# Converting float64 weights on two engines: the sign is carried by the scaled upper word and merged by one two-operand pass

## The chip, the cores and the metric

The kernel runs on one core of a Trainium2 chip. The metric is the device time of one execution in microseconds (us). The kernel before takes 1001.97 us, the median of three runs (1000.22 to 1002.98).

## What is computed

Sliding-window attention (4 batches, 8 heads, 576 positions, head size 64, window 64), and behind it two gated feed-forward layers over all 2304 tokens. The attention inputs are float32, or are used as such; the six weight matrices arrive as float64.

```python
scores = scale * np.matmul(q, k.transpose(0, 1, 3, 2))
mask = (rel >= 0) & (rel < 64)                    # rel = query position - key position
attn = softmax(np.where(mask, scores, -1e9))
x = (attn @ v) as 2304 tokens x 512
x = (silu(x @ w_gate) * (x @ w_val)) @ w_out      # 512 -> 1536 -> 512
x = (sigmoid(x @ w_gate2) * (x @ w_val2)) @ w_out2
```

## The kernel before

Tokens are cut into five tiles of 4, 3, 4, 4 and 3 blocks of 128. The main loop runs over ten passes: the five tiles through the first layer, then the same tiles through the second. Each pass walks the hidden dimension in 12 chunks `fc` of 128, and each chunk is three steps of the TensorE: the gate product into `g` (line 429), the value product into `v` (line 429), and the output product of the chunk before into the accumulators `a` (line 441). Every product is made of three float32 products, high times high, low times high and high times low, so each weight chunk exists as two halves, `w[:, 0]` and `w[:, 1]`. A pass over 512 tokens has 36 matmuls to a chunk.

The attention of the first tile runs before the loop, in the order of the string `START`. The attention of each later tile is laid between the steps of the pass before it, one block of 128 tokens each few chunks. Its work on the VectorE is the masking (line 263), the normalisation (lines 292 to 294) and the low half of `x` (line 331).

The weights are converted in 72 chunks of 128 x 512, 36 for each layer. A float64 is two 32-bit words. `load_raw` brings a chunk as 1024 words a partition into a buffer `raw`; the lower and the upper words alternate there. Then:

- `round_a` works on the ScalarE (ACT): line 377 turns the lower words, times 2^-29, into integers (the three bits of mantissa that go over, rounded) and puts them back in their places; line 380 takes the absolute value of the upper words, read as float32, into a contiguous tile `t`.
- `round_b` works on the VectorE (DVE), four passes: line 388 picks the sign from each upper word as 16-bit numbers and writes it into the upper half of the lower word, at a stride of four; line 389 clamps `t`; line 390 shifts `t` left by three as an integer; line 391 adds `t` and the lower words.
- `split_hi` (line 411, ACT) and `split_lo` (line 415, DVE) make the two halves of the weight from `t`.

The order is written out by hand. In the start, `ca`, `cb`, `ch` and `cl` are `round_a`, `round_b`, `split_hi` and `split_lo`. In the loop a table sets at which step a piece is issued. The conversions of the first layer run in the first pass, those of the second layer during the third to sixth passes; each engine works through its own list in that order, and semaphores carry what one waits for. The rows below also name `s` (line 705, gate times value on DVE), `h` (line 707 on ACT, its low half on DVE in line 621), which the output product takes, and `x` (line 328 on ACT, line 331 on DVE), which the products take.

Of the kernel before, what the change touches and what calls it, by code (L numbers as in the profile page):

```python
# [8 lines left out]
FP32 = mybir.dt.float32  # L9
FP32R = mybir.dt.float32r  # L10
INT32 = mybir.dt.int32
UINT32 = mybir.dt.uint32
UINT16 = mybir.dt.uint16
ACTF = mybir.ActivationFunctionType
ALU = mybir.AluOpType
PSUM = bass.MemoryType.PSUM
DRAM = bass.MemoryType.DRAM


F64_LEAST = 2.0 ** -15  # L20
F64_MOST = 122816.0

# [15 lines left out]
def attention_moe_moe(  # L40
# [20 lines left out]
    nc = tc.nc  # L61
# [7 lines left out]
    scale = 1.0 / float(D) ** 0.5  # L69
# [269 lines left out]
    raws = {}  # L339
# [19 lines left out]
        nc.sync.dma_start(out=dst, in_=rows(key))  # L359
        raws[key] = r  # L360

    def words_of(r):
        w = r.rearrange("p (f two) -> p f two", two=2)
        half = r.bitcast(UINT16).rearrange("p (f four) -> p f four", four=4)
        return w[:, :, 0], w[:, :, 1], half[:, :, 1], half[:, :, 3]

# [1 line left out]
    def round_a(key):  # L372
        t = t_p.tile([128, 512], INT32, tag="t", name="t")
        mids[key] = t
        if wide:
            lower, upper, _, _ = words_of(raws[key])
            nc.scalar.activation(  # L377
                out=lower, in_=lower.bitcast(UINT32), func=ACTF.Copy, scale=2.0 ** -29
            )
            nc.scalar.activation(out=t.bitcast(FP32), in_=upper.bitcast(FP32), func=ACTF.Abs)  # L380

    def round_b(key, keep):
        r = raws.pop(key)
        t = mids[key]
        tf = t.bitcast(FP32)
        if wide:
            lower, _, second, fourth = words_of(r)
            nc.vector.tensor_scalar(second, fourth, 0x8000, 0x4000, ALU.bitwise_and, ALU.bitwise_or)  # L388
            nc.vector.tensor_scalar(tf, tf, F64_LEAST, F64_MOST, ALU.max, ALU.min)  # L389
            nc.vector.tensor_scalar(t, t, 3, None, ALU.logical_shift_left)  # L390
            nc.vector.tensor_tensor(out=t, in0=t, in1=lower, op=ALU.add)  # L391
        else:
            nc.vector.tensor_copy(tf, r)
        mids[key] = tf
        if keep:
            d = dram.tile([128, 512], FP32, name=f"k{key[0]}{key[1]}{key[2]}")
            nc.sync.dma_start(out=d, in_=tf)
            kept[key] = d
# [152 lines left out]
    def conv_b(j):  # L551
        round_b(convs[j][1], convs[j][1][1] == "o")
        raw_ahead(j + 1 + 4)

    for j, (s, key) in enumerate(convs[SPLIT_EARLY:], SPLIT_EARLY):
        at(during, s + 1, round_a, key)
        at(during, s + 2, round_b, key, key[0] == 1 or key[1] == "o")
        at(during, s + 2, raw_ahead, j + 1 + 4)
        if key[0] == 0:
            plan_split(s + 2, key)  # L560
# [32 lines left out]
    for t in range(NTL, 2 * NTL):  # L593
        for fc in range(FC):
            n, key = SPT * t + 3 * fc + 5, (1, "o", fc)
# [29 lines left out]
    with tc.manual_schedule():  # L625
# [4 lines left out]
        t = ps_m.tile([128, 512], FP32, tag="a3", name="warm")  # L630
# [8 lines left out]
        for step in LOADS.split():  # L639
# [31 lines left out]
            "lo": lambda i: x_lo(i, x_of(0), i * 128),  # L671
            "wm": lambda k: warm(k),
            "ca": lambda j: round_a(convs[j][1]),
            "cb": lambda j: conv_b(j),
            "ch": lambda j: split_hi(convs[j][1]),
# [9 lines left out]
        for T in range(2 * NTL):  # L685
            m = T // NTL
            t = ORDER2[T - NTL] if m else T
            n = TILES[t][1]
            for fc in range(FC):
# [7 lines left out]
                    out=s, in_=gps[:, 0:n], func=(ACTF.Silu, ACTF.Sigmoid)[m]  # L697
# [54 lines left out]
```

## Time and profile before

| | |
|---|---|
| median of three runs | 1001.97 us |
| the profiled execution | 1002.0 us, of which the span from the first to the last instruction is 1000.2 us |
| TensorE (PE) busy | 980.4 us, 98% of the span |
| VectorE (DVE) busy | 515.6 us, 52% |
| ScalarE (ACT) busy | 457.0 us, 46% |
| mean granted TensorE clock | 0.986 |
| the four conversion passes on DVE, 72 of each | 54.0 + 33.3 + 30.8 + 49.8 us busy |
| the two conversion passes on ACT, 72 of each | 47.9 + 47.9 us busy |

Busy time is the sum of durations, and neighbours on one engine can overlap: an instruction may be recorded as started before the one ahead of it has ended. The share over the whole span hides stages: in the 40 slices of the page, DVE stands at nine tenths in the second to fifth slice (about 25 to 125 us) and at two to three tenths in the second half. What a pass costs is therefore read in the stage in which it stands, from start to start.

### The profile page before, as it was taken

What the parts mean: (1) busy time and instruction counts of PE and PEld (TensorE: products, weight loads), DVE (VectorE), ACT (ScalarE), POOL (GpSimd) and SP (SyncE); (2) the same over time, 40 slices, a digit from 0 to 9 for tenths busy, and PEclk for the clock granted to TensorE, in tenths of its full rate; (3) what the DMA queues carried; (4) which work ended last, traced back from release to release, by engine and by line L of the source; (5) the groups of instructions that cost most, each with busy time, mean ns of one, the idle gap of its engine ahead of it and who ended that gap; (6) DMA issues with size and microseconds to landing.
All of it is one profiled execution on the core that took longest, in us unless ns stands there. A gap on an engine that the chain in (4) does not pass through costs nothing.

```text
span 1000.2 us, 14684 instructions
## 1 busy us (share of the span) xinstructions
PE 980.4 (98%) x5621; PEld 844.7 (84%) x5621; DVE 515.6 (52%) x1181; ACT 457.0 (46%) x981; POOL 4.1 (0%) x20
## 2 busy tenths in 40 slices
PE   8899999999999999999999999999999999999998
PEld 6678778999888888888999888899988888888997
DVE  6999994545677768666555322233322222223322
ACT  6887785555666555655444222222222222222222
POOL 1000000000000000000000000000000000000000
PEclk7999999999999999999999999999999999999999
DMA  9658797962366667464554400020020002000100
GB/s 224 193 179 221 216 240 171 223 148 80 116 212 186 209 206 232 164 205 137 200 148 126 169 0 1 1 85 1 1 74 1 1 1 74 0 1 1 42 1 32
DMA packets 164982, 113.03 MB, mean 113 GB/s; under 512 B 102704, under 2 KB 139568, under 8 KB 164912
## 3 DMA queue, kind: packets, MB, share of 16 engines
q1 hardware_dynamic: 161264, 111.18, 38.4%
q10 hardware_dynamic: 3648, 0.92, 0.4%
q8 instruction: 44, 0.72, 0.3%
q14 instruction: 26, 0.21, 0.1%
HBM read 90.05 MB, written 27.53 MB: 118 GB/s over the span
## 4 chain that ended last, share of the span: by engine, by line
PE 86%; DVE 9%; issue 2%; DMA 1%; ACT 1%; SPq 0%; DVEq 0%
PE a L441 28%; PE g L429 27%; PE v L429 27%; DVE raw L388 2%; PE att L318 1%; DVE t L390 1%; PE att L244 1%; PE att L302 1%; DVE t L391 1%; DVE t L389 1%; DVE z L263 1%; DVE h L621 1%; DVE s L705 1%; DMA raw<-in_moe_w_val_dram 1%; DVE wv L415 0%
## 5 line engine op out<-in xcount | busy, mean ns | idle before, releaser
L429 PE MATMUL g<-x,wg 128*128 128x512 f32 (+1 forms) x1440 | 317.8, 369 | 0.7 <-ACT x L328 0.7
L429 PE MATMUL v<-x,wv 128*128 128x512 f32 (+1 forms) x1440 | 317.6, 369 | 0.0
L429 PEld LDWEIGHTS g<-x,wg 128*128 128x128 f32 x1440 | 263.3, 188 | 37.5 <-ACT x L328 0.8
L429 PEld LDWEIGHTS v<-x,wv 128*128 128x128 f32 x1440 | 261.1, 188 | 33.1
L705 DVE TENSOR_TENSOR s<-s,v 128x512 f32<-128x512 f32 (+1 forms) x120 | 75.9, 632 | 318.3 <-PE v L429 305.9
L696 ACT ACTIVATE s<-g 128x512 f32<-128x512 f32 (+1 forms) x120 | 66.5, 554 | 312.9 <-PE g L429 312.7
L441 PE MATMUL a<-h,wo 128*128 128x512 f32 (+1 forms) x720 | 166.4, 380 | 6.4 <-DVE h L621 6.4
L441 PE MATMUL a<-wo,h 128*128 128x512 f32 x648 | 157.4, 390 | 0.0
L441 PEld LDWEIGHTS a<-h,wo 128*128 128x128 f32 x720 | 132.3, 192 | 27.0 <-DVE h L621 7.6
L707 ACT ACTIVATE h<-s 128x512 fp32r<-128x512 f32 (+1 forms) x120 | 70.6, 588 | 180.6 <-DVE s L705 180.6
L441 PEld LDWEIGHTS a<-wo,h 128*128 128x128 f32 x648 | 121.3, 188 | 24.2
L621 DVE TENSOR_TENSOR h<-s,h 128x512 fp32r<-128x512 f32 (+1 forms) x120 | 76.1, 634 | 3.2
L388 DVE TENSOR_SCALAR raw<-raw 128x512 uint16<-128x512 uint16 x72 | 54.0, 750 | 9.0 <-ACT raw L377 9.0
L279 ACT ACTIVATE z<-z,nm 128x128 f32<-128x128 f32 x144 | 55.8, 389 | 2.9 <-DVE nm L263 2.7
L101 DVE TENSOR_TENSOR x<-rx,x 128x512 fp32r<-128x512 f32 (+1 forms) x20 | 12.8, 639 | 84.3 <-ACT x L100 84.3
L391 DVE CUSTOM_DVE_ANT_0 t<-raw,t 128x1024 uint16<-128x1024 uint16 x72 | 49.8, 692 | 2.5
L380 ACT ACTIVATE t<-raw 128x512 f32<-128x512 f32 x72 | 47.9, 666 | 0.0
L377 ACT ACTIVATE raw<-raw 128x512 int32<-128x512 uint32 x72 | 47.9, 666 | 0.0
L415 DVE TENSOR_TENSOR wo<-stay,wo 128x512 fp32r<-128x512 f32 x60 | 41.1, 684 | 0.0
L411 ACT ACTIVATE wo<-stay 128x512 fp32r<-128x512 f32 x60 | 37.4, 624 | 0.0
L415 DVE TENSOR_TENSOR wo<-tw,wo 128x512 fp32r<-128x512 f32 x48 | 32.9, 685 | 5.7 <-ACT wo L411 5.7
L389 DVE TENSOR_SCALAR t<-t 128x512 f32<-128x512 f32 x72 | 33.3, 463 | 0.0
(84 smaller groups left out, 562.7 us busy)
## 6 DMA issues: line engine op xcount, KB each, us to landing
raw<-in_moe_w_gate_dram SPq DMA_DIRECT2D x24, 512.0 KB, 4.2
raw<-in_moe_w_val_dram SPq DMA_DIRECT2D x24, 512.0 KB, 4.4
raw<-in_moe_w_out_dram SPq DMA_DIRECT2D x24, 512.0 KB, 3.8
tw<-k0o SPq DMA_DIRECT2D x48, 256.0 KB, 4.2
v<-in_v_dram SPq DMA_DIRECT2D x29, 256.0 KB, 4.5
out_dram<-o SPq DMA_DIRECT2D x18, 256.0 KB, 2.3
k<-ks SPq DMA_DIRECT2D x10, 384.0 KB, 5.3
k0o<-t SPq DMA_DIRECT2D x12, 256.0 KB, 2.2
```

What stands on the lines that cost most here:

```text
L279: nc.scalar.activation(out=z[:, hp, :], in_=z[:, hp, :], func=ACTF.Exp, scale=-1.0, bias=nm[:, hp:hp + 1], accum_out=su[:, hp:hp + 1],)
L377: nc.scalar.activation(out=lower, in_=lower.bitcast(UINT32), func=ACTF.Copy, scale=2.0 ** -29)
L380: nc.scalar.activation(out=t.bitcast(FP32), in_=upper.bitcast(FP32), func=ACTF.Abs)
L388: nc.vector.tensor_scalar(second, fourth, 0x8000, 0x4000, ALU.bitwise_and, ALU.bitwise_or)
L391: nc.vector.tensor_tensor(out=t, in0=t, in1=lower, op=ALU.add)
L415: nc.vector.tensor_tensor(out=w[:, 1], in0=mids.pop(key), in1=w[:, 0].bitcast(FP32), op=ALU.subtract)
L429: nc.tensor.matmul(out=ps[:, 0:n], lhsT=w[:, a, c, :], rhs=xt[:, b, c, 0:n], start=(j == 0), stop=(j == len(mm) - 1),)
L441: nc.tensor.matmul(out=acc[e][:, 0:n] if m == 0 else acc[e], lhsT=w[:, a, cols] if m == 0 else h[:, a, cols], rhs=h[:, b, 0:n] if m == 0 e ...
L621: nc.vector.tensor_tensor(out=h[:, 1, 0:n], in0=s, in1=h[:, 0, 0:n].bitcast(FP32), op=ALU.subtract)
L696: nc.scalar.activation(out=s, in_=gps[:, 0:n], func=(ACTF.Silu, ACTF.Sigmoid)[m])
L705: nc.vector.tensor_tensor(out=s, in0=s, in1=vps[:, 0:n], op=ALU.mult)
L707: nc.scalar.activation(out=h[:, 0, 0:n], in_=s, func=ACTF.Copy)
```

## The change

The upper words are no longer stripped of their sign on ACT. They are copied times 2^-112, read as float32, so that the sign bit stays in `t`; this pass now comes first. The lower words, times 2^-29, go to the first 512 words of the `raw` buffer, contiguous (they lie over upper words that the pass before has read). On DVE the pass on 16-bit halves is gone. The clamp comes first, with bounds of both signs; then one `scalar_tensor_tensor` takes the sign bit of `t` and merges it into the lower words; shift and add follow as before. Six instructions on two engines to a chunk before, six now.

```diff
-F64_LEAST = 2.0 ** -15
-F64_MOST = 122816.0
+F64_MOST = 122816.0 * 2.0 ** -112
...
         if wide:
-            lower, upper, _, _ = words_of(raws[key])
+            r = raws[key]
+            words = r.rearrange("p (f two) -> p f two", two=2)
             nc.scalar.activation(
-                out=lower, in_=lower.bitcast(UINT32), func=ACTF.Copy, scale=2.0 ** -29
+                out=t.bitcast(FP32), in_=words[:, :, 1].bitcast(FP32), func=ACTF.Copy, scale=2.0 ** -112
             )
-            nc.scalar.activation(out=t.bitcast(FP32), in_=upper.bitcast(FP32), func=ACTF.Abs)
+            nc.scalar.activation(
+                out=r[:, 0:512], in_=words[:, :, 0].bitcast(UINT32), func=ACTF.Copy, scale=2.0 ** -29
+            )
...
         if wide:
-            lower, _, second, fourth = words_of(r)
-            nc.vector.tensor_scalar(second, fourth, 0x8000, 0x4000, ALU.bitwise_and, ALU.bitwise_or)
-            nc.vector.tensor_scalar(tf, tf, F64_LEAST, F64_MOST, ALU.max, ALU.min)
+            low = r[:, 0:512]
+            nc.vector.tensor_scalar(tf, tf, -F64_MOST, F64_MOST, ALU.max, ALU.min)
+            nc.vector.scalar_tensor_tensor(low, t, -(2 ** 31), low, ALU.bitwise_and, ALU.bitwise_or)
             nc.vector.tensor_scalar(t, t, 3, None, ALU.logical_shift_left)
-            nc.vector.tensor_tensor(out=t, in0=t, in1=lower, op=ALU.add)
+            nc.vector.tensor_tensor(out=t, in0=t, in1=low, op=ALU.add)
```

On DVE, in the first pass of the loop ahead of the first `h` that an output product waits for, the list reads as follows before (ISA is the integer add; the names in brackets are the semaphores that the row waits for, `DVE_49` being DVE's own and `Activation_49` ACT's).

```order
L415 TENSOR_TENSOR wg<-t,wg 128x512 [waits Activation_49]
L388 TENSOR_SCALAR raw<-raw 128x512 [waits DMAHW1_49,Activation_49]
L389 TENSOR_SCALAR t<-t 128x512 [waits Activation_49]
L390 TENSOR_SCALAR t<-t 128x512 [waits DVE_49]
L391 ISA t<-raw,t 128x1024 [waits DVE_49]
L621 TENSOR_TENSOR h<-s,h 128x512
L415 TENSOR_TENSOR wv<-t,wv 128x512 [waits DMAHW4_49,Activation_49]
```

The same place of DVE's list now (lines have moved up by five, and those above the conversion by two):

```order
L410 TENSOR_TENSOR wg<-t,wg 128x512 [waits Activation_49]
L383 TENSOR_SCALAR t<-t 128x512 [waits Activation_49]
L384 SCALAR_TENSOR_TENSOR raw<-t,raw 128x512 [waits DMAHW1_49,DVE_49,Activation_49]
L385 TENSOR_SCALAR t<-t 128x512 [waits DVE_49]
L386 ISA t<-t,raw 128x1024 [waits DVE_49]
L616 TENSOR_TENSOR h<-s,h 128x512
L410 TENSOR_TENSOR wv<-t,wv 128x512 [waits DMAHW4_49,Activation_49]
```

Before, the second of the four passes waits for nothing on DVE; the third waits for the second and the fourth for the third. Now the merge (line 384) waits for the clamp (383), the shift (385) for the merge, whose input it writes over, and the add (386) for the shift. The neighbours stand where they stood.

On ACT, in the same chunk (a little earlier in time, since ACT runs ahead), before:

```order
L707 ACTIVATE h<-s 128x512 [waits DVE_49]
L411 ACTIVATE wg<-t 128x512
L377 ACTIVATE raw<-raw 128x512 [waits DMAHW1_49,Activation_49]
L380 ACTIVATE t<-raw 128x512
L411 ACTIVATE wv<-t 128x512 [waits DVE_49]
```

And now:

```order
L702 ACTIVATE h<-s 128x512 [waits DVE_49]
L406 ACTIVATE wg<-t 128x512
L370 ACTIVATE t<-raw 128x512 [waits DMAHW1_49]
L373 ACTIVATE raw<-raw 128x512 [waits Activation_49]
L406 ACTIVATE wv<-t 128x512 [waits DVE_49]
```

The two passes have changed places, and the second of them (line 373) now waits for the first one's end, since it writes over words that the first one reads. The lists of PE and of the DMA queues keep their order.

## Rows read from the trace of the kernel before

**Rows 1.** The chain that ended last, from the page: shares of the span by engine

```profile
PE 86%; DVE 9%; issue 2%; DMA 1%; ACT 1%; SPq 0%; DVEq 0%
```

**Rows 2.** Busy time by stretch (us and, in brackets, instructions)

```profile
core 0: us, PE busy (x) PEld busy (x) DVE busy (x) ACT busy (x) POOL busy (x), PEclk, DMA share, GB/s
25.00:45.00 20.00, 15.59 (x205) 12.60 (x204) 19.44 (x54) 16.88 (x47) 0.00 (x0) 0.89 0.68 202
45.00:149.20 104.20, 97.06 (x561) 77.25 (x559) 100.92 (x235) 85.96 (x179) 0.00 (x0) 0.97 0.76 210
...
250.00:480.00 230.00, 229.92 (x1422) 188.78 (x1421) 164.32 (x400) 137.57 (x302) 0.00 (x0) 1.00 0.59 186
480.00:1000.20 520.20, 516.33 (x2502) 455.73 (x2500) 165.41 (x270) 147.27 (x272) 0.00 (x0) 1.00 0.14 44
```

**Rows 3.** PE in order of time: where it stood idle (in brackets, with the releaser)

```profile
66.03 3.93 PE L441 MATMUL a<-h,wo 128*128 128x512 f32 x10 [2.12 <-DVE h L621]
...
107.62 4.14 PE L441 MATMUL a<-h,wo 128*128 128x512 f32 x10 [2.12 <-DVE h L621]
...
149.21 3.95 PE L441 MATMUL a<-h,wo 128*128 128x512 f32 x10 [2.12 <-DVE h L621]
158.41 0.65 PE L202 MATMUL att<-ident,k 128*128 128x128 f32 x4 [0.84 <-DVE x L331]
```

**Rows 4.** DVE in order of time ahead of the first of these stalls

```profile
62.59 0.69 DVE L415 TENSOR_TENSOR wg<-t,wg 128x512 fp32r<-128x512 f32 x1
63.20 0.74 DVE L388 TENSOR_SCALAR raw<-raw 128x512 uint16<-128x512 uint16 x1
63.72 0.46 DVE L389 TENSOR_SCALAR t<-t 128x512 f32<-128x512 f32 x1
64.22 0.43 DVE L390 TENSOR_SCALAR t<-t 128x512 int32<-128x512 int32 x1
64.68 0.69 DVE L391 CUSTOM_DVE_ANT_0 t<-raw,t 128x1024 uint16<-128x1024 uint16 x1
65.29 0.68 DVE L621 TENSOR_TENSOR h<-s,h 128x512 fp32r<-128x512 f32 x1
```

**Rows 5.** DVE in order of time: idle ahead of an instruction, 25 to 155 us

```profile
47.42 0.69 DVE L705 TENSOR_TENSOR s<-s,v 128x512 f32<-128x512 f32 x1 [0.87 <-ACT kt L217]
...
152.09 0.76 DVE L388 TENSOR_SCALAR raw<-raw 128x512 uint16<-128x512 uint16 x1 [1.14 <-ACT raw L377]
```

**Rows 6.** DVE's groups between 25 and 149.2 us (count, busy us, mean ns, idle before)

```profile
L388 DVE TENSOR_SCALAR raw<-raw 128x512 uint16<-128x512 uint16 x34 | 25.5, 750 | 0.0
L391 DVE CUSTOM_DVE_ANT_0 t<-raw,t 128x1024 uint16<-128x1024 uint16 x34 | 23.5, 692 | 1.2
L389 DVE TENSOR_SCALAR t<-t 128x512 f32<-128x512 f32 x34 | 15.9, 466 | 0.0
L390 DVE TENSOR_SCALAR t<-t 128x512 int32<-128x512 int32 x34 | 14.5, 427 | 1.2
...
L294 DVE TENSOR_TENSOR z<-z,su 128x512 f32<-128x512 f32 x9 | 6.2, 692 | 0.3
```

**Rows 7.** ACT in order of time: one release by DVE, and two conversions

```profile
43.57 0.63 ACT L411 ACTIVATE wg<-t 128x512 fp32r<-128x512 f32 x1 [1.94 <-DVE t L391]
...
59.59 0.68 ACT L377 ACTIVATE raw<-raw 128x512 int32<-128x512 uint32 x1
60.17 0.66 ACT L380 ACTIVATE t<-raw 128x512 f32<-128x512 f32 x1
...
70.85 0.67 ACT L377 ACTIVATE raw<-raw 128x512 int32<-128x512 uint32 x1
71.40 0.66 ACT L380 ACTIVATE t<-raw 128x512 f32<-128x512 f32 x1
```

**Rows 8.** DVE in order of time: the conversion that follows the last of these

```profile
72.50 0.76 DVE L388 TENSOR_SCALAR raw<-raw 128x512 uint16<-128x512 uint16 x1
```

More of the change, by code (lines that the diff above doesn't have):

```diff
@@ L12 @@
 UINT32 = mybir.dt.uint32
-UINT16 = mybir.dt.uint16
 ACTF = mybir.ActivationFunctionType
@@ L360, in load_raw @@
         raws[key] = r
[L362 to L365, printed above, removed]
     def round_a(key):
```

## The prediction

> **What bounds the kernel now.** I read the chain of waits first. PE holds 86% of it, DVE 9%, ACT 1% [rows 1]: somewhere PE runs late behind DVE, and the next view has to say where. The busy times by stretch do [rows 2]. From 250 us on PE is busy without a gap (0.08 us idle of 230, then 3.87 of 520), and DVE has a third of its time or more to spare. Between 25 and 149.2 us it is the other way round: DVE is busy 97% of the time, while PE idles 4.4 us and then 7.1 us, at a granted clock of 0.89 and 0.97. PE's own order of time shows what it idles for [rows 3]: three times 2.12 us for the low half of `h` (line 621), 41.6 us apart. Before each such stall DVE was not waiting, it was working through its list: its only idle piece between 25 and 149.2 us is 0.87 us at 47.42, the next comes at 152.09 [rows 5]. So up to the stall at 149.21 the end of the kernel hangs on the length of DVE's list, and after it on PE alone. 34 conversions of the first layer stand in that stretch [rows 6]; of the 36, the first stands ahead of it and the last behind the stall at 149.21.
>
> **What a conversion takes on DVE now.** The stretch is saturated, so what counts is from start to start, and not the durations. In the conversion ahead of the first stall [rows 4] line 388 starts at 63.20 and the next foreign instruction (line 621) at 65.29: 2.09 us. The mean durations add to 0.750 + 0.466 + 0.427 + 0.692 = 2.335 us [rows 6]. The 0.24 us between the two are overlaps: line 389 waits for nothing on DVE and starts 0.22 us before line 388 ends (63.72 against 63.94), and lines 388 and 621 each start 0.08 us before the end of what is ahead of them. Line 390 and line 391, which wait for a result of DVE, start 0.04 and 0.03 us after it. So the pass on 16-bit halves, the longest by its duration, takes only 0.52 us of the list.
>
> **What it will take.** The three waits are now in a row: merge for clamp, shift for merge, add for shift.
> - Clamp: single input, as before. 0.43 us (the same work in line 390, after a wait) to 0.47 (line 389), and 0.03 to 0.05 to the merge, since the merge waits for two or three semaphores. 0.46 to 0.52; I take 0.49.
> - Merge: no row shows such a pass. Below, it could go like the single-input pass of the same width, 0.427 us; above, at half the rate of the two-input passes. The 692 against 427 ns for the same 512 words say that 256 words more cost 0.265 us; another 512 would cost 0.53, so 1.22 us. The nearest row is line 294, two inputs, 128x512, contiguous out, after a wait: 0.692 [rows 6]. I take that, and 0.03 to the shift: 0.72.
> - Shift: unchanged, 0.427 and 0.03: 0.46.
> - Add: its second input is contiguous now. Below 0.427, above 0.692. Line 391, with the strided input, and line 294, without a stride, both take 692 ns: the stride costs nothing there, so its end gains nothing. 0.692 less the overlap of 0.08: 0.61.
>
> Sum 0.49 + 0.72 + 0.46 + 0.61 = 2.28 us (2.25 to 2.31) against 2.09: 0.19 us more (0.16 to 0.22), though the durations add to less than before. The removed pass overlapped its neighbour; the added one stands between two waits.
>
> No row shows a `scalar_tensor_tensor`. The Trainium skill (VectorE: DVE Perf Modes, Why `tensor_tensor` can't do 2×_2P or 4×) says that the second read port cannot help one tensor while a second tensor occupies it; by its (N+151)/0.96 the merge would be 691 ns, an estimate, and the sum would stay as it is.
>
> **What of it reaches the end.** All of it, if the list has no slack. At 43.57 ACT waits 1.94 us for line 391 of the fifth conversion [rows 7], so these five push on too; there the value product's end and ACT's copy of `k` come close together, and 32 of the 34 may count instead of all. With 34 x 0.185 = 6.3 us (34 x 0.22 = 7.5 above, 32 x 0.15 = 4.8 below). PE's stalls grow by about 12 conversions each 41.6 us, 2.2 us; what they cost the clock is there already behind the last one. The profiled execution took 1002.0 us (span 1000.2, 1.8 outside), the median of the runs 1001.97: 1002.0 + 6.3 = **1008.3 us**.
>
> Edits that I put at nothing:
> - ACT. The second pass now waits for the first. Today line 380 starts 0.10 us before line 377 ends (60.17 against 60.27) [rows 7]; afterwards about 0.03 us behind it: 0.13 us a conversion. Multiply or absolute value, contiguous or strided out: lines 377 and 380 differ in both and have nearly one duration (0.66 to 0.68), so between nothing and a few hundredths less. ACT is busy 86 of 104 us, and DVE is the later one. In the tightest place that I found DVE takes up at 72.50 what ACT finished at 71.52 and 72.06 [rows 7, 8]; the merge comes 0.5 us after the clamp, so 0.13 us more is covered. Without that cover: 34 x 0.13 = 4.4 us.
> - The 36 conversions of the second layer, 36 x 0.185 = 6.7 us, lie where DVE idles 66 of 230 us and PE never waits. Without that cover: up to 6.7 us.
> - Transfers: the queues keep their order; a `raw` buffer is still set free by the add, and DVE waits for no transfer in the stretch.
>
> **Rivals.**
> 1. The durations decide, and the overlaps are only how the trace draws it. Then 0.427 + 0.692 + 0.427 + 0.692 = 2.238 against 2.335: 34 x -0.097 = -3.3 us, 998.7. This is the other side; it decides if no instruction can really begin ahead of the end of the one before. For it: the table of groups, where line 388 is the costliest pass. Against it: starts from 63.20 to 65.29 are 2.09 apart, and these are what a saturated list consists of. 0.05.
> 2. A contiguous two-input pass runs at the rate of line 390. The merge alone at 0.427: 2.02 us a conversion, 34 x -0.07 = -2.4, 999.6. The add too: another -0.265, -11 us, of which PE has some 10 to give in the stretch (7.1 idle, 3% of 104 us by its clock): 992. Against it is line 294, contiguous and at 692. 0.08, of which 0.03 within 0.3%.
> 3. The third wait costs nothing, or PE or ACT holds part of the list up anyway. The shift behind the merge as line 621 behind line 391, 0.08 us early instead of 0.03 late: 0.11 less, 34 x 0.075 = +2.6, 1004.6. Against it are the gaps in rows 4, which tell the waiting from those that don't. The Trainium skill (VectorE: DVE Perf Modes, The DRAIN you can't avoid) reports eight copies that took the same with a wait after each as with one at the end; by that the wait would be free, and the trace here does not agree (0.08 early without a wait, 0.03 late with one). 0.10.
> 4. The merge is dear: half the rate of the other two-input passes, 1.22 us: 34 x 0.715 = +24, 1026. No row has such a pass; every two-input row of 512 words is at 0.68 to 0.69. The Trainium skill (Vector Engine (DVE) Microarchitecture Reference, Points that are easy to get wrong) says that this very instruction with two inputs that are not bf16 halves its throughput, without saying against which rate; read as half of 0.69's rate it is this rival. 0.09.
>
> **How the numbers follow.** The forecast has 0.68, with 1006.8 to 1009.5 as its own range. A measurement of this kernel can tell 0.3%, 3.0 us, from no change. Faster by more: rival 1 (0.05) and the larger part of rival 2 (0.05), 0.10. Within: the rest of rival 2 (0.03) and rival 3 (0.10), 0.13. Slower: the forecast and rival 4, 0.77. The range goes from 1000, below which most of rivals 1 and 2 lie, to 1014, which holds the forecast with ACT's cover or most of the second layer's gone; left out is about 0.2.
>
> **What would show it.** Right: the four passes from start to start at about 2.28 us in the saturated stretch, the merge at 0.69 and the shift 0.03 behind its end; stalls for `h` of about 4 us instead of 2.12; the last one near 155 us; PE gapless afterwards. Wrong: a merge at 0.43 or above 0.8 us; an add under 0.69; a shift that starts before the merge has ended; DVE idle inside the stretch for ACT's second pass; a stall of PE behind 165 us.

## The result and the profile after

The changed kernel took 1013.49 us (median of 5 runs, 1008.02 to 1013.87) against 1001.97 us of the kernel before (median of 5, 1000.22 to 1004.68): a ratio of 1.010, 95% interval 1.0069 to 1.0131. In a second comparison it took 1009.62 us (6 runs, 1008.27 to 1014.12), a ratio of 1.0072 (1.0051 to 1.0093). So it is slower by 0.7 to 1.0%, 6.8 and 11.5 us in the two comparisons; the forecast was 6.3 us. Runs of one and the same kernel lie several us apart here (the kernel before: 999.00 to 1005.51 in 23 runs), so single profiles are compared piece by piece below, and totals by their medians. The profiled execution of the changed kernel took 1013.49 us (span 1011.7).

The time of a run goes with the clock that TensorE was granted in it. Of the runs beside the experiments, the kernel before took 999.0 to 1000.3 us in the eight at a mean granted clock of 0.993, and 1002.0 to 1005.5 in the thirteen at 0.984 to 0.986. The changed kernel took 1008.0 to 1008.4 in three runs at 0.993, and 1013.5 to 1014.1 in four at 0.983 to 0.985. At either clock the change costs about 9 us; the 11.5 and 6.8 us are differences of medians over runs of mixed clocks.

The lines have moved: the clamp is line 383, the merge 384, the shift 385, the add 386 (391 before); on ACT the upper words are line 370 (380 before), the lower words 373 (377 before). The product with `x` is line 424 and the one with `h` line 436.

First the saturated stretch by busy time, in the profile after; the answer to [rows 2]. Columns: stretch, its length, busy time (an overlap counted once) and instructions of each engine, granted clock, DMA share, GB/s.

```profile
core 0: us, PE busy (x) PEld busy (x) DVE busy (x) ACT busy (x) POOL busy (x), PEclk, DMA share, GB/s
25.00:45.00 20.00, 13.35 (x187) 10.60 (x186) 17.48 (x50) 16.30 (x46) 0.00 (x0) 0.84 0.64 178
45.00:159.00 114.00, 103.41 (x578) 80.96 (x577) 106.86 (x239) 90.99 (x180) 0.00 (x0) 0.95 0.72 198
250.00:480.00 230.00, 229.15 (x1451) 188.64 (x1450) 166.40 (x398) 143.05 (x304) 0.00 (x0) 1.00 0.57 178
```

The stretch up to the last stall now ends at 159 instead of 149.2 us. DVE is busy 107 of 114 us in it, PE idles 10.6 us instead of 7.1. In the row of the second layer PE idles 0.85 of 230 us where it idled 0.08 before; I come back to that.

DVE's groups in the profile after from 25 to 159 us, the answer to [rows 6] (count, busy us, mean ns, idle before):

```profile
L384 DVE SCALAR_TENSOR_TENSOR raw<-t,raw 128x512 int32<-128x512 int32 x34 | 23.6, 693 | 2.8
L386 DVE CUSTOM_DVE_ANT_0 t<-t,raw 128x1024 uint16<-128x1024 uint16 x34 | 23.5, 692 | 1.2
L385 DVE TENSOR_SCALAR t<-t 128x512 int32<-128x512 int32 x34 | 14.5, 427 | 1.2
L383 DVE TENSOR_SCALAR t<-t 128x512 f32<-128x512 f32 x34 | 14.3, 421 | 0.0
```

The merge takes 693 ns, the clamp 421 instead of 466 (it no longer starts while the pass ahead of it is running), shift and add what they took. The four means add to 2.233 us, 0.10 less than the 2.335 of before. By this view alone the kernel would be faster.

DVE in order of time in the profile after, ahead of the first stall, the answer to [rows 4] (start, duration, line, operation, tiles):

```profile
67.84 0.42 DVE L383 TENSOR_SCALAR t<-t 128x512 f32<-128x512 f32 x1
68.35 0.69 DVE L384 SCALAR_TENSOR_TENSOR raw<-t,raw 128x512 int32<-128x512 int32 x1
69.08 0.43 DVE L385 TENSOR_SCALAR t<-t 128x512 int32<-128x512 int32 x1
69.54 0.69 DVE L386 CUSTOM_DVE_ANT_0 t<-t,raw 128x1024 uint16<-128x1024 uint16 x1
70.15 0.68 DVE L616 TENSOR_TENSOR h<-s,h 128x512 fp32r<-128x512 f32 x1
```

From 67.84 to 70.15 it is 2.31 us; the mean of the 34 conversions is 2.30 against 2.10 before. Every pass but the last now starts after the end of its predecessor: the merge 0.09 us behind the clamp (68.35 against 68.26), the shift 0.04 behind the merge, the add 0.03 behind the shift. Nothing is left of the 0.22 us by which the clamp used to start ahead of the end of the removed pass.

PE in order of time in the profile after, where it stood idle (in brackets, with the releaser), the answer to [rows 3]:

```profile
29.87 1.98 PE L316 MATMUL a<-pt,v 128*64 128x64 f32 x32 [2.56 <-DMA v<-in_v_dram]
...
41.06 1.15 PE L316 MATMUL a<-pt,v 128*64 128x64 f32 x32 [2.19 <-DVE x L329]
42.91 4.61 PE L424 MATMUL g<-x,wg 128*128 128x512 f32 x12 [0.70 <-ACT x L326]
...
70.89 4.63 PE L436 MATMUL a<-h,wo 128*128 128x512 f32 x10 [2.32 <-DVE h L616]
...
115.02 3.95 PE L436 MATMUL a<-h,wo 128*128 128x512 f32 x10 [2.32 <-DVE h L616]
...
159.03 4.14 PE L436 MATMUL a<-h,wo 128*128 128x512 f32 x10 [2.33 <-DVE h L616]
168.42 0.66 PE L200 MATMUL att<-ident,k 128*128 128x128 f32 x4 [0.84 <-DVE x L329]
```

The three stalls for `h` are there, 44.1 us apart instead of 41.6: 2.5 us more, 12 conversions by 0.2. But they are 2.3 us long, against 2.1 before, not 4 us. Between the last two of them the rest went into smaller stalls (for `z` and `h`, such as 0.55 us for `z` at 67.47, ahead of the first one): PE idles 4.3 us instead of 2.4. Between the first two it idles 3.2 us and is busy 1.8 us longer, at a granted clock of 0.93 instead of 0.96. And two things were not foreseen. At 29.87 PE waits 2.56 us for a transfer of `v`. At 42.91 twelve matmuls of the first product take 4.61 us; before the same row is 3.06 us long. The granted clock of that piece is 0.50, the 1.2 GHz level; in the profile before it is 1.00, 2.4 GHz, where this product runs:

```profile
43.00:46.40 3.40, 3.40 (x8) 2.69 (x9) 3.30 (x7) 1.18 (x3) 0.00 (x0) 0.50 0.67 214
```

```profile
40.80:44.20 3.40, 3.40 (x19) 2.81 (x20) 3.33 (x8) 1.46 (x3) 0.00 (x0) 1.00 0.73 230
```

(Above the profile after, below the one before. In 3.4 us, eight of the twelve matmuls run above; below all twelve do, and seven short ones of the attention.)

The half clock reaches DVE's list. Ahead of line 700 at 51.27 DVE idles 2.15 us, where its one idle piece before was 0.87 us. Line 700 reads `v`, the value product behind the slow one, which ran from 48.15 to 51.16. (The view names line 373 on ACT, which ended at 51.21, but line 700 reads nothing of it.)

I set the k-th of the 5621 matmuls of one profile beside the k-th of the other and read how late it starts. The delay of the changed kernel is 2.26 us ahead of the last attention product of the start (38.80 before, 41.06 after), 3.66 us once the first expert product has run, 9.81 us at the last stall for `h`, 10.0 at 265 us, 11.44 at 457 us and 11.49 at the end. So 11.5 us = 2.3 (start) + 1.4 (first product at half clock) + 6.15 (the list from there to the last stall) + 0.2 + 1.45 (second layer). These are two executions; how far two profiles of the same passes can differ, the experiments show.

ACT in the profile after explains the transfer (ACTq is the part of ACT that issues its DMAs):

```profile
21.67 0.66 ACT L370 ACTIVATE t<-raw 128x512 f32<-128x512 f32 x1
22.37 0.69 ACT L373 ACTIVATE raw<-raw 128x512 int32<-128x512 uint32 x1
22.37 0.72 ACTq L116 DMA_DIRECT2D v<-in_v_dram  x1
```

And in the profile before:

```profile
19.65 0.39 ACT L279 ACTIVATE z<-z,nm 128x128 f32<-128x128 f32 x1
19.68 0.73 ACTq L118 DMA_DIRECT2D v<-in_v_dram  x1
...
21.67 0.66 ACT L377 ACTIVATE raw<-raw 128x512 int32<-128x512 uint32 x1
22.22 0.66 ACT L380 ACTIVATE t<-raw 128x512 f32<-128x512 f32 x1
```

Before, the load of `v` was issued at 19.68, while ACT was still in the exponentials, though the passes of lines 377 and 380 stand ahead of it in the program. Now the lower words' pass writes over words that the upper words' pass reads, so it waits for that pass; the load stands behind it in the program and is issued only when the wait is over, at 22.37: 2.7 us later. On top of that it took 7.4 us to land in this execution, 4.1 before (from issue to landing, by the DMA issues).

### The profile page after: what moved, and what is told of

It reads as the page before. It is cut to its first block, busy times and chain, and to the rows that moved or that the text cites. A ratio compares the mean times of both kernels' runs of the same rounds, so it can differ in the third digit from the quotient of the medians.

```text
span 1011.7 us, 14670 instructions
## 1 busy us (share of the span) xinstructions
PE 985.5 (97%) x5621; PEld 847.0 (84%) x5621; DVE 523.8 (52%) x1181; ACT 466.1 (46%) x981; POOL 4.1 (0%) x20
## 4 chain that ended last, share of the span: by engine, by line
PE 65%; DVE 1%; ACT 0%; issue 0%; DVEq 0%
PE a L436 22%; PE g L424 21%; PE v L424 21%; PE att L316 0%; PE att L242 0%; PE att L300 0%; DVE raw L384 0%; DVE t L385 0%; DVE kt L229 0%; DVE t L383 0%; DVE s L700 0%; DVE h L616 0%; ACT raw L373 0%; DVE qt L229 0%; ACT o L453 0%
## 5 line engine op out<-in xcount | busy, mean ns | idle before, releaser
L384 DVE SCALAR_TENSOR_TENSOR raw<-t,raw 128x512 int32<-128x512 int32 x72 | 49.9, 693 | 8.6 <-ACT raw L373 3.3
L386 DVE CUSTOM_DVE_ANT_0 t<-t,raw 128x1024 uint16<-128x1024 uint16 x72 | 49.9, 693 | 2.5
L383 DVE TENSOR_SCALAR t<-t 128x512 f32<-128x512 f32 x72 | 30.2, 420 | 9.0 <-ACT t L370 9.0
```

The lines of the kernel that those rows point to most:

```text
L384: nc.vector.scalar_tensor_tensor(low, t, -(2 ** 31), low, ALU.bitwise_and, ALU.bitwise_or)
L386: nc.vector.tensor_tensor(out=t, in0=t, in1=low, op=ALU.add)
```

## The experiments

In dispute after the result: whether starts or durations make the list's length (rival 1); whether the third wait has a price (rival 3); whether the late load and the half clock belong to the change or to the execution; what the second layer's part is; and whether contiguity gives anything. Each expectation was written before its run.

**The load of `v` ahead of the passes.** The list that sets the order at the start, changed kernel; `vp0` (the load) stands before `ca1` (the two ACT passes):

```
-... wo0 wm2 ca1 no2 ne1 tq3 vp0 po1 ...
+... wo0 wm2 vp0 ca1 no2 ne1 tq3 po1 ...
```

> The changed kernel, with one step of the start moved: the load of v for block 0, which stands in ACT's list, is issued ahead of the second conversion's two ACT passes instead of behind them. Theory A (ACT's new wait between its two passes holds up what is queued behind it, and so delays this transfer by 2.7 us): the transfer is issued near 19.7 us instead of 22.37, PE's 2.56 us wait for v at 29.87 goes, DVE's idle 1.72 us at 32.52 shrinks to under 0.5, a conversion stays at 2.25 to 2.31 us from start to start, the last stall for h moves from 159.0 to about 157, and the time falls from 1013.5 by 1.5 to 2.7 us, to about 1011.3. Rival B (the late transfer was chance of that one execution, or the delay is absorbed before the last stall): the last stall stays within 0.5 us of 159.0 and the time within 0.5 us of 1013.5.

1011.19 us (6 runs, 1010.73 to 1012.74), ratio to before 1.0091 (1.0064 to 1.0118). The load was issued at 18.01, and PE had no stall for it. A conversion still took 2.305 us; the delay at the last stall was 7.0 us (156.22) instead of 9.8, at the end 9.3. So the piece-by-piece figures came about as expected (the stall was forecast near 157). The first product ran at half clock here too, from 40.9 to 44.2 us. Whether the median of the changed kernel loses these 2.3 us is another question, which the repeat below answers.

**Lower words in place.** The contiguous layout undone, the rest kept:

```
-                out=r[:, 0:512], in_=words[:, :, 0].bitcast(UINT32), func=ACTF.Copy, scale=2.0 ** -29
+                out=words[:, :, 0], in_=words[:, :, 0].bitcast(UINT32), func=ACTF.Copy, scale=2.0 ** -29
...
-            low = r[:, 0:512]
+            low = r.rearrange("p (f two) -> p f two", two=2)[:, :, 0]
```

> The changed kernel, but the lower words are put back in their own places (every second word) as before, so that ACT's second pass writes over nothing that the first one reads; the merge and the add then read them at a stride of two. Theory A: ACT's wait is gone, its passes overlap by 0.10 us again, the transfer of v is issued near 19.7 us and its stall goes; merge and add stay at 0.69 us, a conversion at 2.25 to 2.31; 1010 to 1012 us. Rival C (contiguous words do make DVE's two-input passes cheaper, and the stride costs): merge or add above 0.72 us, a conversion above 2.35 us, and 34 of them cost more than the transfer gives back: 1014 or more.

1010.69 us (1007.99 to 1012.24), ratio 1.0084 (1.0056 to 1.0112). ACT's two passes overlap again, and the load of `v` is issued at 18.25. On DVE the merge and the add read every other word of `raw`:

```profile
L384 DVE SCALAR_TENSOR_TENSOR raw<-t,raw 128x512 int32<-128x512 int32 x34 | 23.6, 694 | 2.8
L386 DVE CUSTOM_DVE_ANT_0 t<-raw,t 128x1024 uint16<-128x1024 uint16 x34 | 23.6, 693 | 1.2
```

694 and 693 ns strided, 693 and 692 contiguous: the contiguous words buy nothing on DVE, while they bring ACT its wait.

**The third wait taken away.** The shift writes to the free half of `raw`, not over the words that the merge reads, so it need not wait for the merge:

```
+            u = r[:, 512:1024]
-            nc.vector.tensor_scalar(t, t, 3, None, ALU.logical_shift_left)
+            nc.vector.tensor_scalar(u, t, 3, None, ALU.logical_shift_left)
-            nc.vector.tensor_tensor(out=t, in0=t, in1=low, op=ALU.add)
+            nc.vector.tensor_tensor(out=t, in0=u, in1=low, op=ALU.add)
```

> The changed kernel, but the shift writes to the upper half of the raw buffer instead of over its input t, so that it no longer waits for the merge; the add reads it there. Theory A: the shift starts 0.08 us before the merge ends instead of 0.03 behind it, a conversion takes 2.14 to 2.20 us instead of 2.25 to 2.31, 34 times 0.11 is 3.7 us, and the time falls to about 1009.8 us, the stall for v at 29.87 staying. Rival B (a wait between two DVE passes costs nothing): 2.25 to 2.31 us a conversion, and the time within 0.5 us of 1013.5.

1006.19 us (12 runs, 1002.95 to 1008.49), ratio 1.0044 (1.0026 to 1.0062). DVE in order of time in this kernel:

```profile
63.00 0.42 DVE L383 TENSOR_SCALAR t<-t 128x512 f32<-128x512 f32 x1
63.51 0.69 DVE L384 SCALAR_TENSOR_TENSOR raw<-t,raw 128x512 int32<-128x512 int32 x1
64.12 0.42 DVE L386 TENSOR_SCALAR raw<-t 128x512 int32<-128x512 int32 x1
64.58 0.69 DVE L387 CUSTOM_DVE_ANT_0 t<-raw 128x1024 uint16<-128x1024 uint16 x1
65.19 0.68 DVE L617 TENSOR_TENSOR h<-s,h 128x512 fp32r<-128x512 f32 x1
```

The shift starts 0.08 us before the merge has ended (64.12 against 64.20), and a conversion takes 2.19 us: 0.11 less than with the wait, with all durations unchanged. That is the price of this wait, and rival 3 falls. The Trainium skill (VectorE: DVE Perf Modes, The DRAIN you can't avoid) reports eight copies that took the same with a wait after each of them as with one at the end. Here the trace does not agree, one wait costs 0.11 us. The total is 3.6 us below the expected one, which the waits alone do not explain: the second layer lost 0.34 us instead of 1.45, and the profiled execution had no half clock in the first product.

**The kernel before with clamp and sign pass exchanged.** The four instructions stay; only which passes stand next to each other changes. The sign pass, which waits for nothing on DVE, now stands between the clamp and the shift that waits for it:

```
-            nc.vector.tensor_scalar(second, fourth, 0x8000, 0x4000, ALU.bitwise_and, ALU.bitwise_or)
             nc.vector.tensor_scalar(tf, tf, F64_LEAST, F64_MOST, ALU.max, ALU.min)
+            nc.vector.tensor_scalar(second, fourth, 0x8000, 0x4000, ALU.bitwise_and, ALU.bitwise_or)
```

> The kernel before, with the first two DVE passes of a conversion exchanged: clamp, sign on 16-bit halves, shift, add; the same four instructions. Theory A (starts count, not durations): the shift finds its clamp long done, so only the add still waits for what is just ahead of it; a conversion takes 1.94 to 2.00 us from start to start instead of 2.09, 34 times -0.12 is -4 us, about 998 us. Rival B (durations count): no change, 1002 within 1 us.

998.98 us (12 runs, 996.19 to 1003.93), ratio 0.997 (0.9948 to 0.9991): a little faster than before. DVE in order of time:

```profile
61.03 0.42 DVE L388 TENSOR_SCALAR t<-t 128x512 f32<-128x512 f32 x1
61.37 0.73 DVE L389 TENSOR_SCALAR raw<-raw 128x512 uint16<-128x512 uint16 x1
61.89 0.46 DVE L390 TENSOR_SCALAR t<-t 128x512 int32<-128x512 int32 x1
62.38 0.69 DVE L391 CUSTOM_DVE_ANT_0 t<-raw,t 128x1024 uint16<-128x1024 uint16 x1
62.99 0.69 DVE L621 TENSOR_TENSOR h<-s,h 128x512 fp32r<-128x512 f32 x1
```

1.96 us here and 1.99 in the mean, instead of 2.10, while the durations still add to 2.336 us (the 0.47 that the clamp had behind the 16-bit pass is now the shift's). 34 x 0.11 = 3.7 us; measured 0.3% or 3.0 us, 2.3 between the medians. In the profile PE reaches the last stall 5.2 us earlier than in the profile before, and 3.7 us earlier than in the one further down that has the old passes in the first layer; behind it PE then waits 1.5 us for a transfer of `q`. So rival 1 is refuted on the kernel before itself: the same sum of durations in another order gives another time, and it follows the starts.

**The changed kernel again,** unaltered, to see which of its delays come back:

> The changed kernel once more, unaltered, beside the others on one chip, for the transfer of v. Theory A (it is late in most executions because ACT's wait holds it up): issued within 0.05 us of the start of ACT's second pass (line 373), 2 us or more later than in the run that issues it ahead, PE waits for it, and the median is above that run's 1011.2 us by 1 to 2.5. Rival B (chance): no such wait, and the same 1011 us as the runs in which the transfer was issued early.

1009.62 us, ratio 1.0072 (1.0051 to 1.0093); the profiled execution 1008.37. ACT and its DMA issue in this profile:

```profile
21.11 0.67 ACT L373 ACTIVATE raw<-raw 128x512 int32<-128x512 uint32 x1
21.12 0.71 ACTq L116 DMA_DIRECT2D v<-in_v_dram  x1
```

and PE:

```profile
27.34 1.98 PE L316 MATMUL a<-pt,v 128*64 128x64 f32 x32
...
38.53 1.15 PE L316 MATMUL a<-pt,v 128*64 128x64 f32 x32 [2.19 <-DVE x L329]
40.38 3.02 PE L424 MATMUL g<-x,wg 128*128 128x512 f32 x12 [0.70 <-ACT x L326]
```

The load again starts only with line 373, so the late issue belongs to the change. But it landed in 3.6 us, and PE did not wait for it; nor is the first product slow (3.02 us). The delay is 0.04 us at 50 us, 6.05 at the last stall (155.26), 4.63 behind it, 6.32 at 457 us and 6.39 at the end. The drop of 1.4 us behind the last stall is clock: PE runs there at 1.00 in this profile (155.3 to 158.7 us), and at 0.50 in the profile before (148.9 to 152.1) and in the first one of the changed kernel (159.1 to 162.4). What comes back in both profiles is the list from 50 us on (6.0 here, 6.15 there) and the second layer (1.4 in both). The stall at the start and the half clock of the first product came in one profile of the two. The half clock is no chance of that execution alone, though: over all runs, five of the eight profiles with new passes in the first layer have it, and none of the three with the old ones. Nor do the medians show the load's 2.3 us: the ratio here, 1.0072, isn't above the 1.0091 of the kernel that loads `v` earlier. And the earlier start of that kernel's profile is not the moved load's doing: it is 0.33 us ahead of the profile before at the last attention product, and this profile, with the late load, is 0.27 ahead. I had put the stall down to the late load alone; in these two profiles it came where a late load and a slow transfer met.

**The new passes in the second layer alone.** Both passes' code stands side by side, chosen by the layer:

```
+            if key[0] == 1:
+                low = r[:, 0:512]
+                nc.vector.tensor_scalar(tf, tf, -F64_SMALL, F64_SMALL, ALU.max, ALU.min)
...
+            else:
+                lower, _, second, fourth = words_of(r)
...
```

> The kernel before for the 36 conversions of the first layer, the changed passes for the 36 of the second. My prediction put those at nothing, since DVE idles there; the trace of the changed kernel shows PE losing about 1.5 us between 265 and 460 us. Theory A (bursts of attention and conversions hold up attention's small PE steps although DVE has time on average): PE as before up to 260 us, 1.0 to 1.8 us lost by 460, about 1003 us. Rival B (those 1.5 us are the later arrival of what the first layer put off, or chance): under 0.4 us lost between 265 and 460, the time as before.

1004.06 us (10 runs, 1000.69 to 1005.37), ratio 1.0015 (0.9999 to 1.0032). The total alone is too near to no change to tell. Matmul by matmul the delay grows from -2.73 us at 265 to -1.32 at 457 us: 1.4 us lost between them, as in both profiles of the changed kernel. The -2.73 shows how far two profiles of the same passes can lie apart, for the first layer here is that of the kernel before. What PE waits for in this stretch (engine, tile and line, releaser: us in total, times, longest):

```profile
PE att L245 <- DVE kt L232: 0.6, 2, 0.4
PE att L303 <- DVE z L295: 0.3, 1, 0.3
```

The same view of the profile before has no row for PE at all. These are not conversions but the attention's own work, which stands on DVE behind a conversion that is longer now. PE's weight loads wait as well: 2.5 us in total for `h` and `raw` of ACT between 265 and 460 us, where those of the profile before wait 0.4 us for ACT.

And the conversions are longer here by more than the 0.2 us of the first layer. Where DVE takes a conversion up as soon as ACT has delivered, the merge has to wait for ACT's second pass; in the profile after:

```profile
273.71 0.43 DVE L383 TENSOR_SCALAR t<-t 128x512 f32<-128x512 f32 x1 [0.99 <-ACT t L370]
274.41 0.69 DVE L384 SCALAR_TENSOR_TENSOR raw<-t,raw 128x512 int32<-128x512 int32 x1 [0.28 <-ACT raw L373]
```

From 250 to 480 us this comes 11 times, 2.7 us in total. With the lower words in place, where ACT's second pass has no wait of its own, the merge starts there 0.14 us behind the clamp, and the second layer lost 0.8 us and not 1.4. So ACT's new wait has a part in this loss, by these profiles nearly half; no run changed it alone.

**Three passes.** What follows from the above: fewer passes in a row. On the kernel with the lower words in place, ACT's scale and bias for the lower words keep their result within three bits (`LOW_SCALE` is 2^-29 less one part in 2^20; the bits below are cut off and not rounded), so that an `or` does in place of the `add`, and the shift goes into one pass with it:

```
-                out=words[:, :, 0], in_=words[:, :, 0].bitcast(UINT32), func=ACTF.Copy, scale=2.0 ** -29
+                out=words[:, :, 0], in_=words[:, :, 0].bitcast(UINT32), func=ACTF.Copy, scale=LOW_SCALE, bias=-0.5
...
-            nc.vector.scalar_tensor_tensor(low, t, -(2 ** 31), low, ALU.bitwise_and, ALU.bitwise_or)
-            nc.vector.tensor_scalar(t, t, 3, None, ALU.logical_shift_left)
-            nc.vector.tensor_tensor(out=t, in0=t, in1=low, op=ALU.add)
+            nc.vector.scalar_tensor_tensor(low, t, 3, low, ALU.logical_shift_left, ALU.bitwise_or)
+            nc.vector.scalar_tensor_tensor(t, t, -(2 ** 31), low, ALU.bitwise_and, ALU.bitwise_or)
```

> From the run with the lower words in place: the three bits of mantissa are cut off instead of rounded (ACT's second pass subtracts a half), so that shift and merge can be one bitwise pass: clamp, (t shifted left by 3) or lower, (sign of t) or that. Three DVE passes instead of four, each waiting for the one ahead, and no ACT wait. Theory A (start to start: 0.50 + 0.73 + 0.61): a conversion takes 1.84 us against 2.10 before, 34 times -0.26 is -8.8 us of DVE's list by 149 us; PE has idled 7 us there and lost 3% of its clock, so most but not all of it counts: 994 to 997 us against 1001 to 1002 before. Rival B (durations count: 0.42 + 0.69 + 0.69 = 1.80 against 2.335, -18 us of list, all that PE can give): about 991.

995.71 us (6 runs, 994.21 to 997.91), ratio 0.9929 (0.9913 to 0.9945); on another chip 994.52 (993.78 to 997.41), ratio 0.993 (0.9906 to 0.9953). It beats both kernels. DVE in order of time:

```profile
59.99 0.42 DVE L384 TENSOR_SCALAR t<-t 128x512 f32<-128x512 f32 x1
60.50 0.69 DVE L385 SCALAR_TENSOR_TENSOR raw<-t,raw 128x512 int32<-128x512 int32 x1
61.23 0.69 DVE L386 SCALAR_TENSOR_TENSOR t<-t,raw 128x512 int32<-128x512 int32 x1
61.84 0.16 DVE L291 TENSOR_SCALAR su<-su 128x4 f32<-128x4 f32 x1
```

1.85 us for this conversion and 1.87 in the mean, 0.23 less than before; 34 of them make 7.9 us, of which 7.1 arrive. PE's waits show where the rest stays:

```profile
66.04 2.57 PE L436 MATMUL a<-h,wo 128*128 128x512 f32 x10 [1.15 <-DVE h L616]
...
151.61 0.63 PE L201 MATMUL att<-ident,q 128*128 128x128 f32 x4 [2.17 <-DMA q<-in_q_dram]
```

The stalls for `h` have shrunk to 1.15 us and less, and at the end of the stretch PE comes to a transfer of `q` that has not landed.

**Two passes.** The same without the clamp (what is left out: the bound on overlarge weights), to see how far the list can shrink before it no longer counts:

> From the run with three passes, the clamp left out (so weights too large for float32 would not be held at the largest value; these inputs have none): two DVE passes a conversion. The question is where the list stops to decide. If DVE were the bound all the way, 1.34 instead of 1.84 us a conversion would give 34 times 0.5, 17 us. Theory A (PE is the bound as soon as the list has room): PE idled 0.7 to 1.2 us at each of three stalls for h with three passes, and then 2.2 us for the transfer of q near 152 us; the stalls for h go, a wait for transfers or for ACT stays, and the time falls by 1 to 4 us only, to 992 to 995. Rival B (the list still decides): under 985.

992.63 us (4 runs, 991.44 to 993.88), ratio 0.9907 (0.9883 to 0.9931), beside the 994.52 of the three passes on the same chip. 34 x 0.5 us of clamp would have been 17; 1.9 us came. From 45 to 145 us, two passes and then three:

```profile
45.00:145.00 100.00, 99.98 (x621) 81.57 (x621) 83.22 (x179) 86.82 (x183) 0.00 (x0) 1.00 0.81 224
```

```profile
45.00:145.00 100.00, 97.04 (x575) 77.89 (x574) 93.53 (x208) 86.93 (x181) 0.00 (x0) 1.00 0.80 222
```

With two passes PE is busy for 99.98 of 100 us and DVE idles 17: the list is not the bound any more.

## Why the prediction was right, and where it was not

- **What bounds the kernel.** Right. DVE's list up to the last stall for `h` sets the end; exchanging two passes, taking a wait away or a whole pass each moved the time by about the list's change, until PE was full (two passes).
- **Starts, not durations.** Right, and shown by the exchanged passes: an unchanged sum of durations, 0.11 us a conversion less.
- **The merge at the rate of line 294.** Right: 0.693 against 0.692 taken. Rival 2 (0.427) and rival 4 (1.22) fell.
- **The gaps.** The term was a little too small. Behind the clamp I put 0.03 to 0.05 us; it was 0.09, so a conversion grew by 0.20 where I took 0.185. 34 x 0.20 = 6.8 instead of 6.3. From 50 us on, where 29 of the 34 stand (5.8 us), the list grew by 6.0 and 6.15.
- **The second layer at nothing.** Wrong by 1.4 us, shown in both profiles of the changed kernel and by the run with the new passes in that layer alone. The cover that I named (DVE idles 66 of 230 us) is a mean. The few attention steps that PE waits for stand behind conversions, and there the cover is shorter.
- **ACT at nothing.** Wrong in the second layer. I called ACT's 0.13 us covered because the merge comes 0.5 us after the clamp; in 11 conversions of the second layer the merge waited 0.28 us for ACT's second pass.
- **"Transfers: the queues keep their order", at nothing.** Wrong as a mechanism. The order stays, but a wait of an engine also holds the DMA issues that stand behind it. I counted ACT's new wait as 0.13 us of ACT's time; what it did was to take away the lead of a load, 2.7 us. In one profile that cost 2.3 us, together with a transfer of 7.4 us, in the other nothing.
- **Stalls of 4 us, the last one near 155 us.** The length was wrong (2.3 us): I put the whole growth of 12 conversions into the stall for `h`, but it spread over smaller stalls for `z` and `h` ahead of it and, in one profile, over matmuls at half clock. The last one came at 159.0 and at 155.3 us: the second is the forecast, the first has the 3.7 us of the start and of the first product on top.
- **A stall of PE behind 165 us** I had named as a sign of being wrong, and it came: 0.9 us in the second layer. DVE also idled inside the saturated stretch, 1.72 us at 32.52 and 2.15 at 51.27 in the first profile, but for `x` behind the late `v` and, by what line 700 reads, for PE's late product, not for ACT's second pass.

What the change costs is better read against the run with the new passes in the second layer alone, whose first layer is that of the kernel before and whose granted clock (0.993) is that of the repeat (0.992). Against it the repeat's matmuls start 1.3 us later at the last attention product of the start, 7.55 us later at the last stall and 7.6 at 265 us; with the 1.45 us of the second layer that is 9.1, as the runs at equal clock have it. So the first layer costs 7.6 us where I forecast 6.3, and the second 1.45 where I put nothing. Of the 7.6 us, 6.8 are 34 conversions by 0.20; no run splits the other 0.8. That the second comparison gave 6.8 us, so near the forecast, is in part luck with the clocks of the runs compared. The first one's 11.5 has in its profile the late load (2.3 us) and the half clock of the first product (1.4).

What sets that clock stays open. In the five profiles with the half clock in the first product, PE had idled 1.9 to 2.2 us ahead of the last attention product before it; in the four where it idled 1.3 us or less the clock was full. But in two it idled 2.1 and 2.2 us and the clock was full too (the repeat is one of them), so this idle time alone does not decide it. No run was made to settle this, nor whether the change makes the lower clock more frequent.

## What to carry to other kernels

In a saturated list read from start to start: a pass that waits for nothing just ahead of it may cost far less than its duration, and a pass between two waits costs all of it and the gaps too. Put an independent pass between two that depend on each other, or fold two into one; and when a change makes an engine wait for itself, look at the DMA issues that stand behind that wait, and at what waits for the later result. An engine that is idle a third of the time on average can still be late at the few places where it is waited for.

## What the runs showed of the hardware

- The longest pass by its duration was not the dearest: 16-bit halves at every fourth place took 0.75 us, but the next pass began after 0.52 (0.22 us before the end), while behind 32-bit passes the lead was 0.08 us, so that the add with its 0.69 took 0.61.
- Two-input passes on 128x512 words took 680 to 694 ns whatever they did: bitwise `scalar_tensor_tensor`, integer add, f32 product, contiguous or every other word.
- A wait for one earlier pass put the start 0.03 to 0.04 us behind that pass's end; where the merge waits for three semaphores it is 0.09 (no run tells whether their number makes the difference).
- ACT's DMA issue ran up to 2 us ahead of ACT's own work (19.68 against the pass at 21.67), but not past a wait that ACT's program has ahead of it (22.37 with the pass itself).
